# A gated recurrence with a capped choice of experts: exponentials moved ahead of the last decay, register loads in parts of 16 and 8, products in gaps, front and zeros rearranged

## The chip, the cores and the metric

One core of one Trainium2 chip runs the whole program. The metric is device time in microseconds of one execution. The kernel before has a median of 233.89 us over 3 runs (233.44 to 235.4).

## The reference

Two blocks follow each other. The first is a recurrence over 5056 steps for 4 batches and 256 channels, the second a layer of 8 experts of which each keeps the 80 tokens with the largest gate weight; all other rows of the output are zero.

```python
sig = 1 / (1 + exp(-f_logit)); f = lower_bound + (1 - lower_bound) * sig
for t in range(S):                       # S = 5056, h is (4, 256)
    h = f[:, t] * h + (1 - f[:, t]) * x[:, t];  y[:, t] = h
x = y.reshape(20224, 256)
logits = x @ w_gate                      # (20224, 8)
expert = argmax(logits); gate = softmax(logits)[expert]
for e in range(8):                       # the 80 best tokens of expert e
    tok = tokens of e with the 80 largest gate
    out[tok] = gate[tok] * (relu(x[tok] @ w1[e]) @ w2[e])   # 256 -> 1024 -> 256
```

All arithmetic is float32. The inputs x and f_logit are 20.7 MB each, the expert weights 16.8 MB, the output 20.7 MB.

## The kernel before, in words

**The loop.** The sequence is cut into 10 groups of 512 steps (the last has 448), and each group into 4 units, one per batch: 40 units. For each unit SyncE's queue (SP) loads 512 KB of f_logit and 512 KB of x into one of 4 buffers each, three units ahead (`load`, L243). ScalarE (ACT) takes the sigmoid in place (`gate`, L252), GpSimd (POOL) multiplies x with it (`enter`, L256), TensorE (PE) transposes both to channels (`to_channels`, L263), ACT makes the decay from the transposed sigmoid (`decay`, L273), and VectorE (DVE) runs the recurrence as a scan (`scan`, L281) into `h_all`, which holds all states in SBUF, channels down the partitions. PE makes the gate logits of the unit before (`logits`, L296). When the 4 units of a group are done, ACT copies its logits out of PSUM (`aside`, L304), PE turns them to tokens (`by_token`, L310), DVE subtracts the maximum (`maxima`) and marks the chosen expert (`choice`, the last step of which, L337, is on POOL). The four engines work through these steps in the order in which the program writes them; each engine's instructions run in order, and nothing is reordered. Each DMA that SP issues uses one of eight semaphores in turn and waits for the DMA eight before it.

**The zeros.** The output has to be zero where no token is kept. One megabyte of zeros is written to a scratch tensor (`z_dram`, `spread_zeros`, L240), from where SP copies it to the output in quarters of a chunk (32 partitions x 2048 numbers, 256 KB, `clear_some`, L164): 14 quarters in the loop, 6 behind the last load, 30 between the first six weight loads and 30 behind the other weight loads, 80 in all.

**The choice of tokens.** After the loop the shifted logits are exponentiated and summed (`exponentials` L343, `halved` L357, `sums` L349), the gate weight's reciprocal is put in a list per expert (`worth` L371, `turned` L377, `candidates` L383), and the best 12 of each of 128 lists are found (`peaks` L388, `vals` L536 and L539). A product with `spread` (`rivals`, L549) lets every candidate be compared with those of the other lists (`signs` L559 on ACT, `beat` L578 on DVE); those with less than 80 above them are kept, and their places in `h_all` are written to `trow` (L605), one row of 80 numbers per expert. `busy` (L178) issues products of the identity with itself, whose result nobody reads: 16 behind `rivals` and 22 behind `kept`.

**The gathers.** For each expert three engines share the 80 tokens (`gather`, L664 and L669): each loads some numbers of the expert's row of `trow` into registers with one TENSOR_LOAD per part, and then copies, number by number, 2 x 4 bytes per partition from `h_all` to `xe`. DVE then scales `xe` to `xt` (`scaled`, L677). The parts before are 18 and 16 on DVE, 14 and 14 on ACT, 18 on POOL.

**The experts.** Each expert has 8 pieces of `hidden` (two products each, L701) and 8 of `result` (L716), the latter 6 pieces behind; ACT applies the relu per half expert (L710), DVE scales the result (L731), POOL scatters it to the output (L734). The weights are loaded in halves of 512 KB (32 of them) into a ring of 6 buffers: SP issues the next when PE has used one up, and with it 1 or 2 quarters of zeros (`more`). The scatters wait until all zeros are issued.

Of the kernel before, what the change touches and what calls it, by code (L numbers as in the profile page):

```python
# [35 lines left out]
def kernel(  # L36
# [56 lines left out]
    lb = consts.tile([P, DC], F32, name="lb")  # L93
    nc.scalar.dma_start(out=lb, in_=lower_bound.rearrange("(o p) -> p o", p=P))
# [3 lines left out]
    nc.scalar.dma_start(out=wg[:, :, :E], in_=w_gate.rearrange("(o p) e -> p o e", p=P))  # L98
# [54 lines left out]
    z_dram = dram.tile([P, ZR * D], F32, name="z_dram")  # L153
# [4 lines left out]
    zeros = [(k, q) for k in clears for q in range(ZQ)]  # L158


    def clear(k, q=0, m=ZQ):
        n = min(ZR, N // P - k) * D
        rows = ds(q * QP, m * QP)
        nc.sync.dma_start(out=out_z[rows, ds(k * D, n)], in_=z_dram[rows, :n])  # L164
# [34 lines left out]
    with tc.tile_pool(name="ld", bufs=4) as ld, \  # L199
# [6 lines left out]
        def setup():  # L206
# [26 lines left out]
            nc.vector.tensor_scalar(omlb, lb, -1.0, 1.0, ALU.mult, ALU.add)  # L233
            nc.vector.tensor_scalar(nomlb, lb, 1.0, -1.0, ALU.mult, ALU.add)
            for o in range(DC):
                nc.vector.tensor_scalar_mul(wg[:, o], wg[:, o], omlb[:, ds(o, 1)])

        def spread_zeros():
            m = ZR * D // ZC
            nc.sync.dma_start(out=z_dram.rearrange("p (m z) -> p m z", m=m),  # L240
                              in_=zero.unsqueeze(1).broadcast_to([P, m, ZC]))
# [162 lines left out]
        LAST = n_unit - 1  # L404

        for n in range(-AHEAD, n_unit):
            unit(load, n + AHEAD)
            if n == -1:
                spread_zeros()
# [7 lines left out]
            if n == LAST - 2:  # L417
                aside(OLD)
            elif n == LAST - 1:
                exponentials(0, OLD)  # L420
            unit(scan, n)
            some_of(of_group, 1)
            unit(logits, n - 1)
            if n + AHEAD == LAST:
                clear_some(6)
            elif B <= n < n_unit - 2 * B and n % 2:
                clear_some(1)
            if n > 0 and n % B == 0:
# [19 lines left out]
        candidates(HALF)
# [11 lines left out]
        turned(g, 1, fresh[:, ds(NP * TOP + P, P)])  # L460
        for k in (2, OLD - 2, HALF):
# [71 lines left out]
    with tc.tile_pool(name="sel", bufs=1) as sel:  # L533
# [18 lines left out]
        busy(psu, 16, "up")  # L552
# [307 lines left out]
```

## Time and profile before

| | us |
|---|---|
| median of 3 runs | 233.89 |
| runs | 233.44 to 235.4 |
| profiled execution: its own time | 233.3 |
| its span, first to last instruction | 231.5 |
| busy PE / DVE / ACT / POOL | 191.3 / 156.0 / 134.4 / 130.6 |
| mean granted clock of PE | 0.934 |
| moved by DMA | 81.58 MB, mean 352 GB/s |

Times in the rows below are from the start of the span. A row of the timeline has the start, the time from the first to the last of the merged instructions, the engine, the line, the operation, the tiles (out <- in), the count, and in brackets how long the engine was idle before and what ended that. PE's weight loads (PEld) run beside its products. A granted clock of 1.00 is 2.4 GHz, 0.50 is 1.2 GHz.

### The profile page before, as it was taken

The numbers are of one execution on the slowest core, as the hardware profiler recorded it, in microseconds if no ns is written. First come the engines' busy times: TensorE is split into PE (matmuls) and PEld (weight loads), VectorE is DVE, ScalarE is ACT, GpSimd is POOL, SyncE is SP. The second block draws the span as 40 slices with busy tenths as digits, with TensorE's granted clock in tenths as the row PEclk, the third lists the DMA queues.
The fourth block names the chain that finished last, engine by engine and source line by source line (L and its number), as shares of the span: only waits on it lengthen the run. The fifth ranks groups of instructions, "written<-read, shape, count | busy, mean of one in ns | idle before, by whom it ended". The sixth has DMA issues, their size and how long they took to land.

```text
span 231.5 us, 5464 instructions
## 1 busy us (share of the span) xinstructions
PE 191.3 (83%) x1825; PEld 160.9 (69%) x1825; DVE 156.0 (67%) x503; ACT 134.4 (58%) x399; POOL 130.6 (56%) x229
## 2 busy tenths in 40 slices
PE   0688999998999999999995619849899799889990
PEld 0676878788787878787874409849778577657860
DVE  5468779998999999999999479342562544253010
ACT  4457879888888888878766307055564165340110
POOL 2359788888989898989783601044434431300731
PEclk9997999999999999999999656995599999999997
DMA  5999999999999999999975999952389999999920
GB/s 165 394 416 420 417 421 418 417 415 418 418 415 423 417 420 418 420 415 420 405 302 195 379 367 367 379 219 77 143 277 395 405 405 405 415 400 401 385 83 25
DMA packets 29188, 81.58 MB, mean 352 GB/s; under 512 B 3296, under 2 KB 11616, under 8 KB 26720
## 3 DMA queue, kind: packets, MB, share of 16 engines
q1 hardware_dynamic: 28224, 80.49, 88.5%
q0 software_dynamic: 384, 0.66, 0.9%
q8 instruction: 16, 0.26, 0.4%
q14 instruction: 20, 0.16, 0.2%
q10 hardware_dynamic: 544, 0.01, 0.1%
HBM read 79.44 MB, written 22.41 MB: 440 GB/s over the span
## 4 chain that ended last, share of the span: by engine, by line
DMA 38%; PE 28%; ACT 10%; DVE 7%; issue 6%; POOL 5%; DVEq 2%; ACTq 0%; POOLq 0%; SPq 0%
DMA f_t<-in_f_logit_dram 17%; DMA out_dram<-z_dram 7%; PE sp L263 7%; DMA w_sb<-in_moe_w_dram 7%; PE y_ps L716 5%; PE lg L296 5%; ACT h_all L273 4%; DMA x_t<-in_x_dram 4%; DVE xe L669 4%; PE up L263 3%; PE h_ps L701 3%; POOL x_t L256 3%; DMA wg<-in_moe_w_gate_dram 3%; ACT f_t L252 3%; PE warm L178 2%
## 5 line engine op out<-in xcount | busy, mean ns | idle before, releaser
L256 POOL TENSOR_TENSOR x_t<-f_t,x_t 128x1024 f32<-128x1024 f32 x39 | 92.3, 2375 | 19.4 <-DMA x_t<-in_x_dram 16.1
L281 DVE TENSOR_TENSOR_SCAN h_all<-h_all,up 128x512 f32<-128x512 f32 (+1 forms) x80 | 94.7, 1241 | 5.8 <-ACT h_all L273 4.3
L273 ACT ACTIVATE h_all<-sp,nomlb 128x512 f32<-128x512 f32 (+1 forms) x80 | 50.1, 676 | 14.2 <-PE sp L263 14.1
L263 PE MATMUL sp<-ident,f_t 128*128 128x128 f32 x320 | 46.1, 289 | 7.0 <-ACT f_t L252 5.8
L701 PEld LDWEIGHTS h_ps<-xt,w_sb 128*128 128x128 f32 x256 | 40.3, 208 | 14.1 <-DVE xt L677 4.5
L252 ACT ACTIVATE f_t<-f_t 128x1024 f32<-128x1024 f32 x40 | 42.5, 1062 | 12.1 <-DMA f_t<-in_f_logit_dram 12.1
L263 PE MATMUL up<-ident,x_t 128*128 128x128 f32 x320 | 43.6, 281 | 4.3 <-POOL x_t L256 2.6
L263 PEld LDWEIGHTS sp<-ident,f_t 128*128 128x128 f32 x320 | 36.5, 146 | 15.1 <-issue 12.5
L669 DVE COPY xe<-h_all 128x8 uint8 x272 | 22.0, 164 | 34.6 <-issue 34.6
L701 PE MATMUL h_ps<-xt,w_sb 128*128 128x80 f32 x256 | 40.0, 287 | 5.9 <-DVE xt L677 3.9
L263 PEld LDWEIGHTS up<-ident,x_t 128*128 128x128 f32 x320 | 37.1, 144 | 6.6 <-POOL x_t L256 4.5
L716 PE MATMUL y_ps<-w_sb,hid 128*80 128x256 f32 x128 | 38.6, 392 | 3.7 <-issue 1.7
L669 POOL COPY xe<-h_all 128x8 uint8 x144 | 19.4, 195 | 36.6 <-issue 17.8
L669 ACT COPY xe<-h_all 128x8 uint8 x224 | 23.7, 193 | 23.7 <-issue 23.5
L296 PE MATMUL lg<-h_all,wg 128*32 128x128 f32 (+1 forms) x640 | 26.9, 285 | 4.5 <-ACT ls L304 2.9
L296 PEld LDWEIGHTS lg<-h_all,wg 128*32 128x32 f32 x640 | 15.6, 109 | 11.7 <-ACT ls L304 4.8
L734 POOL DMA_INDIRECT out_dram<-y,goal x8 | 7.5, 938 | 20.8 <-DMA w_sb<-in_moe_w_dram 15.2
L710 ACT ACTIVATE hid<-h_ps 128x320 f32<-128x320 f32 x16 | 6.9, 433 | 21.1 <-PE h_ps L701 17.7
L716 PEld LDWEIGHTS y_ps<-w_sb,hid 128*80 128x80 f32 x128 | 15.1, 156 | 5.5 <-issue 3.2
L731 DVE TENSOR_SCALAR y<-y_ps,gsl 80x256 f32<-80x256 f32 x8 | 3.8, 476 | 12.5 <-PE h_ps L701 8.0
L178 PEld LDWEIGHTS warm<-ident 128*128 128x128 f32 x76 | 10.3, 220 | 0.1
L178 PE MATMUL warm<-ident 128*128 128x128 f32 x76 | 10.4, 303 | 0.0
(125 smaller groups left out, 97.3 us busy)
## 6 DMA issues: line engine op xcount, KB each, us to landing
f_t<-in_f_logit_dram SPq DMA_DIRECT2D x40, 512.0 KB, 6.6
x_t<-in_x_dram SPq DMA_DIRECT2D x40, 512.0 KB, 7.0
w_sb<-in_moe_w_dram SPq DMA_DIRECT2D x32, 512.0 KB, 7.7
out_dram<-z_dram SPq DMA_DIRECT2D x31, 256.0 KB, 7.0
out_dram<-z_dram SPq DMA_DIRECT2D x10, 512.0 KB, 9.0
out_dram<-z_dram SPq DMA_DIRECT2D x4, 1024.0 KB, 15.1
out_dram<-z_dram SPq DMA_DIRECT2D x3, 768.0 KB, 9.1
z_dram<-zero SPq DMA_DIRECT2D x1, 1024.0 KB, 8.9
```

What stands on the lines that cost most here:

```text
L178: nc.tensor.matmul(warm, ident, ident, start=True, stop=True)
L252: nc.scalar.activation(s_t, s_t, ACT.Sigmoid, scale=-1.0)
L256: (nc.gpsimd if n else nc.vector).tensor_tensor(u_t, sts[n], u_t, ALU.mult)
L263: nc.tensor.transpose(at, src[n][:, r, ds(o * P, P)], ident)
L273: nc.scalar.activation(columns(n, o).rearrange("c (p r) -> c p r", r=R), sps.pop((n, o)).rearrange("c (r p) -> c p r", r=R) [:, lead(n // ...
L281: nc.vector.tensor_tensor_scan(h, h, ups.pop((n, o))[:, lead(n // B):], columns(n - B, o)[:, size(n // B - 1) - 1:] if n >= B else 0.0, AL ...
L296: nc.tensor.matmul(lgs[g][ds(r * LC, LC), b, :k], wg[:, o], h[:, r], start=o == 0, stop=o == DC - 1, skip_group_check=True)
L669: copy(xe[:, :, ds(WORD * (k + j), WORD)], pair(v - HOME))
L701: nc.tensor.matmul(HP[e, i][:, c], w[1, e, i][:, o, ds(c * P, P)], XT[e][:, o], start=o == 0, stop=o == DC - 1, skip_group_check=True)
L710: nc.scalar.activation(HID[e][:, ds(i * CH, CH)], HP.pop((e, i)), ACT.Relu)
L716: nc.tensor.matmul(YP[e], HID[e][:, c], w[2, e, c // CH][:, c % CH], start=c == 0, stop=c == FC - 1)
L734: one = nc.gpsimd.indirect_dma_start(out=out, out_offset=bass.IndirectOffsetOnAxis(ap=goal[:, ds(e, 1)], axis=0), in_=Y.pop(e), in_offset= ...
```

## The change

It has six parts. (1) The exponentials of groups 0 to 7 stand ahead of the last unit's decay on ACT, their sums (`halved`) are all on POOL, right behind the last `enter`, the choice of group 8 moves behind the last scan, wholly to DVE, and the copy of the last logits (`aside(9)`) comes ahead of the candidates. (2) `busy` gets 16 more products at the start, 4 ahead of the last `by_token`, 32 behind the last `turned`, and 20 instead of 16 behind `rivals`. (3) The parts of the gathers are 16 and 16 on DVE, 16 and 8 on ACT, 16 and 8 on POOL. (4) `lb` is loaded as two rows of 128 numbers and transposed by PE; `w_gate` is loaded by SP behind the second unit, and scaled behind the first scan. (5) The first megabyte of zeros goes straight to the output and is copied from there; `z_dram` is gone. (6) Of the 76 quarters left 20 are issued in the loop (also behind every unit from 28 to 35), 6 behind the last load, 30 with the first six weights, 20 with the next 16 weights (1, and 2 with every fourth).

```diff
-PAD = 40
+PAD = 48
...
-    lb = consts.tile([P, DC], F32, name="lb")
-    nc.scalar.dma_start(out=lb, in_=lower_bound.rearrange("(o p) -> p o", p=P))
+    lb = consts.tile([DC, P], F32, name="lb")
+    nc.scalar.dma_start(out=lb, in_=lower_bound.rearrange("(o p) -> o p", p=P))
...
-    zeros = [(k, q) for k in clears for q in range(ZQ)]
+    zeros = [(k, q) for k in clears[1:] for q in range(ZQ)]
+
+    def first_zeros(zero):
+        m = ZR * D // ZC
+        nc.sync.dma_start(out=out_z[:, :ZR * D].rearrange("p (m z) -> p m z", m=m),
+                          in_=zero.unsqueeze(1).broadcast_to([P, m, ZC]))
...
-        nc.sync.dma_start(out=out_z[rows, ds(k * D, n)], in_=z_dram[rows, :n])
+        nc.sync.dma_start(out=out_z[rows, ds(k * D, n)], in_=out_z[rows, :n])
...
-            nc.vector.tensor_scalar(omlb, lb, -1.0, 1.0, ALU.mult, ALU.add)
-            nc.vector.tensor_scalar(nomlb, lb, 1.0, -1.0, ALU.mult, ALU.add)
+            busy(psu, 16, "up")
+            lb_t = plg.tile([P, DC], F32, name="lb_t", tag="lt")
+            nc.tensor.transpose(lb_t, lb, ident[:DC, :DC])
+            nc.vector.tensor_scalar(omlb, lb_t, -1.0, 1.0, ALU.mult, ALU.add)
+            nc.vector.tensor_scalar(nomlb, lb_t, 1.0, -1.0, ALU.mult, ALU.add)
+
+        def gates():
             for o in range(DC):
                 nc.vector.tensor_scalar_mul(wg[:, o], wg[:, o], omlb[:, ds(o, 1)])
...
             if n == LAST - 2:
                 aside(OLD)
+                exponentials(0, OLD)
             elif n == LAST - 1:
-                exponentials(0, OLD)
+                for k in range(0, OLD, HALF):
+                    halved(k, HALF)
             unit(scan, n)
-            some_of(of_group, 1)
+            if n == 0:
+                gates()
+            some_of(of_group, 1 if n != LAST - 1 else 0)
...
-            elif B <= n < n_unit - 2 * B and n % 2:
+            elif B <= n < LAST - AHEAD and (n % 2 or n >= n_unit - 3 * B):
                 clear_some(1)
...
-        halved(0, HALF)
-        sums(HALF, OLD)
-        worth(0, 0, 2, nc.gpsimd)
-        candidates(0)
+        aside(g)
+        busy(psu, 4, "up")
+        by_token(g)
+        for k in (0, 2, HALF):
+            worth(k, k // HALF * HALF, 2, nc.gpsimd)
         worth(OLD - 2, HALF, 2, nc.vector)
-        aside(g)
-        worth(2, 0, 2, nc.gpsimd)
-        candidates(2)
-        by_token(g)
-        candidates(OLD - 2)
-        worth(HALF, HALF, 2, nc.gpsimd)
-        candidates(HALF)
+        for k in (0, 2, OLD - 2, HALF):
+            candidates(k)
...
         turned(g, 1, fresh[:, ds(NP * TOP + P, P)])
+        busy(psu, 32, "up")
...
-        busy(psu, 16, "up")
+        busy(psu, 20, "up")
...
-    ways = [(mybir.EngineType.DVE, nc.vector.tensor_copy, [18, 16]),
-            (mybir.EngineType.Activation, nc.scalar.copy, [14, 14]),
-            (mybir.EngineType.Pool, nc.gpsimd.tensor_copy, [K - 62])]
+    ways = [(mybir.EngineType.DVE, nc.vector.tensor_copy, [16, 16]),
+            (mybir.EngineType.Activation, nc.scalar.copy, [16, 8]),
+            (mybir.EngineType.Pool, nc.gpsimd.tensor_copy, [16, K - 72])]
...
-                    clear_some(1 + len(late) % 2)
+                    clear_some(1 + (len(late) % 4 == 0))
```

In the built program `trow` begins at byte 24224 of a partition's memory before, and at byte 24704 after: `lb`, which stands ahead of it, takes 512 bytes where it took 8, rounded up to 32. The row of an expert begins there in the expert's partition, and a part at column k begins 4k bytes further.

Three places show how instructions move. On ACT, at the end of the loop, before (`f_t` is the sigmoid, `h_all` the decay, `ls` the copied logits, `cand` the shifted logits):

```order
L252 ACTIVATE f_t<-f_t 128x1024
L273 ACTIVATE h_all<-sp,nomlb 128x448 x2
L304 COPY ls<-lg 128x512
L273 ACTIVATE h_all<-sp,nomlb 128x448 x2
L343 ACT_TABLE_LOAD
L343 ACTIVATE cand<-cand 128x1024
L343 ACTIVATE cand<-cand 128x128
L383 COPY cand<-ct 128x256
L304 COPY ls<-lg 128x4x112
L383 COPY cand<-ct 128x256 x3
```

and now:

```order
L255 ACTIVATE f_t<-f_t 128x1024
L276 ACTIVATE h_all<-sp,nomlb 128x448 x2
L307 COPY ls<-lg 128x512
L346 ACT_TABLE_LOAD
L346 ACTIVATE cand<-cand 128x1024
L276 ACTIVATE h_all<-sp,nomlb 128x448 x2
L346 ACTIVATE cand<-cand 128x128
L307 COPY ls<-lg 128x4x112
L386 COPY cand<-ct 128x256 x4
```

The large exponential and its table load moved ahead of the last decay, and the last copy of logits ahead of the four copies of candidates. On PE, from the last logits to the first expert, before (`ct` and `fresh` are turned candidates, `warm` the products that nobody reads):

```order
L296 MATMUL lg<-h_all,wg 32x112 x24
L377 MATMUL ct<-ident,gm 128x128 x4
L310 MATMUL lt<-ident,ls 128x128 x4
L377 MATMUL ct<-ident,gm 128x128 x4
L377 MATMUL fresh<-ident,gm 128x128 x2
L549 MATMUL rivals<-spread,mates 128x192 x2
L178 MATMUL warm<-ident 128x128 x16
L586 MATMUL sums_p<-count,before 128x1
L602 MATMUL kept<-put,what 16x80 x12
L178 MATMUL warm<-ident 128x128 x22
```

and now:

```order
L299 MATMUL lg<-h_all,wg 32x112 x24
L181 MATMUL warm<-ident 128x128 x4
L313 MATMUL lt<-ident,ls 128x128 x4
L380 MATMUL ct<-ident,gm 128x128 x8
L380 MATMUL fresh<-ident,gm 128x128 x2
L181 MATMUL warm<-ident 128x128 x32
L555 MATMUL rivals<-spread,mates 128x192 x2
L181 MATMUL warm<-ident 128x128 x20
L592 MATMUL sums_p<-count,before 128x1
L608 MATMUL kept<-put,what 16x80 x12
L181 MATMUL warm<-ident 128x128 x22
```

The turn of the last logits (`lt`) moved ahead of all candidates, and 32 products stand between the last candidates and `rivals`. On POOL, the end of the gathers now reads:

```order
L670 TENSOR_LOAD trow
L675 COPY xe<-h_all 128x2x4 x16
L670 TENSOR_LOAD trow
L675 COPY xe<-h_all 128x2x4 x8
L740 DMA out_dram<-y,goal 20224x256 x4
L670 TENSOR_LOAD trow
L675 COPY xe<-h_all 128x2x4 x16
L670 TENSOR_LOAD trow
L675 COPY xe<-h_all 128x2x4 x8
L740 DMA out_dram<-y,goal 20224x256 x4
```

Before, each expert had one load and 18 copies there, and all eight scatters stood behind the last of them; now four scatters stand ahead of the last expert's gather.

## Rows read from the trace of the kernel before

**Rows 1.** The page: the chain that ended last, share of the span by engine.

```profile
DMA 38%; PE 28%; ACT 10%; DVE 7%; issue 6%; POOL 5%; DVEq 2%; ACTq 0%; POOLq 0%; SPq 0%
```

**Rows 2.** The page: GB/s of the DMA engines in 40 slices of 5.79 us.

```profile
GB/s 165 394 416 420 417 421 418 417 415 418 418 415 423 417 420 418 420 415 420 405 302 195 379 367 367 379 219 77 143 277 395 405 405 405 415 400 401 385 83 25
```

**Rows 3.** Stretches: busy PE, PEld, DVE, ACT, POOL; then PE's clock, DMA share, GB/s.

```profile
130.00:135.00 5.00, 2.51 (x10) 1.52 (x8) 3.37 (x12) 1.22 (x4) 1.88 (x6) 0.50 1.02 363
145.00:150.00 5.00, 4.32 (x48) 4.13 (x47) 1.37 (x6) 0.21 (x1) 0.00 (x0) 1.00 0.99 381
160.00:165.00 5.00, 4.19 (x18) 3.67 (x18) 1.65 (x17) 3.18 (x29) 2.44 (x19) 0.50 0.47 161
```

**Rows 4.** Timeline, SP's queue in the front.

```profile
5.92 0.63 SPq L240 DMA_DIRECT2D z_dram<-zero  x1
```

**Rows 5.** Timeline, ACT and DVE at the end of the loop.

```profile
117.06 1.06 ACT L252 ACTIVATE f_t<-f_t 128x1024 f32<-128x1024 f32 x1 [0.35 <-DMA f_t<-in_f_logit_dram]
119.24 0.59 ACT L304 COPY ls<-lg 128x512 f32<-128x512 f32 x1
121.90 1.16 ACT L273 ACTIVATE h_all<-sp,nomlb 128x448 f32<-128x448 f32 x2 [2.08 <-PE sp L263]
123.08 1.28 ACT L343 ACT_TABLE_LOAD   x1
...
123.90 2.17 DVE L281 TENSOR_TENSOR_SCAN h_all<-h_all,up 128x448 f32<-128x448 f32 x2
...
124.37 1.26 ACT L343 ACTIVATE cand<-cand 128x1024 f32<-128x1024 f32 x2
```

**Rows 6.** Timeline, the choice of tokens.

```profile
128.79 0.54 ACT L304 COPY ls<-lg 128x448 f32<-128x448 f32 x1
...
133.20 0.47 PE L377 MATMUL fresh<-ident,gm 128*128 128x128 f32 x1 [0.56 <-DVE gm L367]
...
138.00 0.36 DVE L544 TENSOR_TENSOR spread<-vals,place 128x192 f32<-128x192 f32 x1
...
138.56 1.62 PE L549 MATMUL rivals<-spread,mates 128*128 128x192 f32 x4 [4.89 <-DVE spread L544]
```

**Rows 7.** Timeline, 22 products (two instructions each) and the write of trow.

```profile
147.71 5.18 PE L178 MATMUL warm<-ident 128*128 128x128 f32 x44
147.82 0.23 DVE L605 TENSOR_SCALAR trow<-kept 8x80 int32<-8x80 f32 x1 [1.33 <-PE kept L602]
```

**Rows 8.** Register loads of line 664: duration ns min/median/max, start; five parts of one row.

```profile
L664 DVEq TENSOR_LOAD <-trow x1: 1573/1573/1573, 173.6 to 173.6; - x1
L664 DVEq TENSOR_LOAD <-trow x1: 3617/3617/3617, 165.9 to 165.9; - x1
L664 ACTq TENSOR_LOAD <-trow x1: 3062/3062/3062, 172.9 to 172.9; - x1
L664 ACTq TENSOR_LOAD <-trow x1: 1217/1217/1217, 162.0 to 162.0; - x1
L664 POOLq TENSOR_LOAD <-trow x1: 4043/4043/4043, 168.7 to 168.7; - x1
```

**Rows 9.** Timeline, the first gathers and the first expert.

```profile
152.62 2.38 POOL L669 COPY xe<-h_all 128x8 uint8 x18 [10.01 <-issue]
...
154.27 1.33 DVE L669 COPY xe<-h_all 128x8 uint8 x16 [2.86 <-issue]
...
156.11 4.93 PE L701 MATMUL h_ps<-xt,w_sb 128*128 128x80 f32 x24 [3.22 <-DVE xt L677]
...
162.92 0.42 ACT L710 ACTIVATE hid<-h_ps 128x320 f32<-128x320 f32 x1
```

**Rows 10.** The chain in order of time: start, us, what; the experts.

```profile
174.63 0.43 PE y_ps L716 x2
175.07 0.40 PE h_ps L701 x4
...
225.29 0.49 DVE y L731
```

More of the change, by code (lines that the diff above doesn't have):

```diff
@@ L97 @@
     nc.vector.memset(wg, 0.0)
-    nc.scalar.dma_start(out=wg[:, :, :E], in_=w_gate.rearrange("(o p) e -> p o e", p=P))
     omlb = consts.tile([P, DC], F32, name="omlb")
@@ L152 @@
     ZC = 512
-    z_dram = dram.tile([P, ZR * D], F32, name="z_dram")
     out_z = out.rearrange("(p k) d -> p (k d)", p=P)
@@ L232, in setup @@
             nc.vector.tensor_tensor(before, before, mates, ALU.mult)
-            nc.vector.tensor_scalar(omlb, lb, -1.0, 1.0, ALU.mult, ALU.add)
-            nc.vector.tensor_scalar(nomlb, lb, 1.0, -1.0, ALU.mult, ALU.add)
+            busy(psu, 16, "up")
[4 more added lines that the diff above has]
+        def gates():
             for o in range(DC):
                 nc.vector.tensor_scalar_mul(wg[:, o], wg[:, o], omlb[:, ds(o, 1)])
[L238 to L241, printed above, removed]
         def load(n):
@@ L404 @@
         LAST = n_unit - 1
+        HALF = OLD // 2
         for n in range(-AHEAD, n_unit):
             unit(load, n + AHEAD)
-            if n == -1:
-                spread_zeros()
+            if n == -2:
+                nc.sync.dma_start(out=wg[:, :, :E], in_=w_gate.rearrange("(o p) e -> p o e", p=P))
+            elif n == -1:
+                first_zeros(zero)
             if n == -AHEAD:
@@ L430 @@
                 of_group += ([[lambda g=g: aside(g)]] if g < OLD else [])
-                of_group += [[lambda g=g: shifted(g)], [lambda g=g: choice(g, nc.gpsimd)]]
+                of_group += [[lambda g=g: shifted(g)], [lambda g=g: choice(g, nc.gpsimd if g < OLD else nc.vector)]]
         assert not of_group
@@ L435 @@
         g = n_grp - 1
-        HALF = OLD // 2
-        halved(0, HALF)
-        sums(HALF, OLD)
-        worth(0, 0, 2, nc.gpsimd)
-        candidates(0)
-        worth(OLD - 2, HALF, 2, nc.vector)
-        aside(g)
-        worth(2, 0, 2, nc.gpsimd)
-        candidates(2)
-        by_token(g)
-        candidates(OLD - 2)
-        worth(HALF, HALF, 2, nc.gpsimd)
-        candidates(HALF)
+        aside(g)
[3 more added lines that the diff above has]
+            worth(k, k // HALF * HALF, 2, nc.gpsimd)
+        worth(OLD - 2, HALF, 2, nc.vector)
+        for k in (0, 2, OLD - 2, HALF):
+            candidates(k)
         assert OLD == 8
@@ L824 @@
             nc.vector.tensor_scalar(trow, rp, float(WORD), float(HOME), ALU.mult, ALU.add)
-            for k in clears:
+            zero = sel.tile([P, ZC], F32, name="zero")
+            nc.vector.memset(zero, 0.0)
+            first_zeros(zero)
+            for k in clears[1:]:
                 clear(k)
```

## The prediction

> **What bounds the kernel now.** I read the chain of waits by engine first [rows 1]: DMA holds 38% of it, PE 28%. The throughput by slices [rows 2] shows two stages in which the 16 DMA engines are the limit (about 418 GB/s from 12 to 110 us, about 400 from 174 to 220) and a hole between (slices of 77 to 302). So the program has three parts with three limits: the loop over 40 units (transfers), the choice of tokens and the first gathers (waits between engines), the experts (PE, held up by transfers). The table of stretches [rows 3] shows PE at 0.50 of its clock (1.2 GHz) in 130 to 135 and 160 to 165, and at 1.00 (2.4 GHz) in 145 to 150. Three marks: A, the end of the copy of group 8's logits, 119.24 + 0.59 = 119.83 [rows 5]; T, the end of the write of `trow`, 147.82 + 0.23 = 148.05 [rows 7]; and the end of PE's work, 225.29, where DVE starts on the last y [rows 10]. From there to the execution's own 233.3 are 8.0 us, which no edit touches. That execution lies 0.6 under the median of 233.89; 1% is 2.3 us, about what the measurement can tell.
>
> **Zeros, loop.** A quarter chunk is 32 x 2048 x 4 B = 0.262 MB. The loop issues 20 of them where it issued 14, the six more in the stretch where the loads run closest; the first megabyte goes to the output in place of `z_dram`, the same bytes. The queue is full there (405 to 423 GB/s from 12 to 116 us [rows 2]), and the sigmoid of the last unit waited 0.35 us for its f_t [rows 5], so nothing hides the bytes: 6 x 0.262 / 0.418 = **+3.8** on A. Bounds: 0 if the compute of those units had the slack, 3.8.
>
> **Front.** The zeros' first write was issued at 5.92 [rows 4], behind the 4-byte pieces of `lb`, whose completion it waited for. `lb` is now two rows of 512 B. The first two slices lack (417 - 165) and (417 - 394) GB/s x 5.79 us = 1.6 MB, 3.8 us, most of it the start itself. I take **-0.5**, between 0 and -1.8. The 16 products and the transpose ahead of the first f_t are PE time while PE waits for the second f_t anyway; up to +1 if the first release of a buffer is late, inside that range. `gates` on DVE moves past two scans: before the first logits, free.
>
> **Exponentials.** Table load and exponential are 1.28 + 1.07 us: 123.08 to 125.4 [rows 5], after the last decay. Now they start at A = 119.83 and end at 122.2; the last decay, ready at 121.90 [rows 5], starts 0.3 late. DVE doesn't feel it: its scan before runs until 123.5, and the last scan, which now doesn't follow the choice of group 8, starts 0.45 us earlier than 123.90 [rows 5]. The table load had no visible gap behind it (1.28 us, the exponential at +1.29). The Trainium skill's page "ScalarE: Activation LUTs", section "What ACT_TABLE_LOAD costs", adds a drain of about 1.38 us to each load, which speaks against the move: by it the last decay would start 1.7 late and the last scan some 0.7 late. The trace shows no such drain behind this load, so the sum goes without.
>
> **Last logits.** Their copy stood at 128.79 [rows 6], behind the exponentials, a POOL sum and another copy, 2.7 us after the last scan's end (126.07). Now it waits for the choice of group 8 on DVE, an exponential of 128 and the last logits: about 0.8 us. But the peaks of the first pair still go ahead on DVE. The transpose that ends the chain moves from 133.20 to about 131.4 [rows 6]: -1.8.
>
> **32 products.** They are put behind that transpose. 22 took 5.18 us at full clock [rows 3, 7], 0.235 each, so 32 take 7.5: 131.6 to **139.1**. `spread` is then ready at 136.6 (138.36 - 1.8) [rows 6], and the product of rivals, queued behind, waits for them: 139.1 instead of 138.56. If PE is at 1.2 GHz for part of it (0.50 in 130 to 135 [rows 3]), up to 142.5; I take 139.9, since PE has four more products and no gap over 1 us until 128.7. From the rivals to T were 9.5 us; 0.8 goes because the rivals' 1.62 us [rows 6] were at half clock. T before the loop's shift: 139.9 + 8.7 = 148.6: **+0.5** (-0.8 to +2.6). Without the wait behind the products it would be -2.
>
> **Register loads.** The decisive part. [Rows 8] give five loads of one expert's row of `trow`: 18 numbers from column 0 in 1.57 us, 16 from 18 in 3.62, 14 from 34 in 3.06, 14 from 48 in 1.22, 18 from 62 in 4.04. That is 0.087 us a number for the first and fourth, 0.22 for the others, whatever the engine or count. The tile began at byte 24224 of its partition; the fast parts begin at bytes that 32 divides (24224, 24416), the slow ones not (24296, 24360, 24472). Now it begins at 24704 (`lb` has grown by 480 bytes), and all parts (columns 0, 16, 32, 48, 56, 72) at bytes that 32 divides. I price all at 0.087: 1.40 for 16, 0.70 for 8. Bounds: 0.087 and 0.225.
>
> First gather: DVE's second load started 0.76 us before its copies were done, so it shows 0.64 where it showed 2.86 [rows 9]. DVE: 1.40 + 0.5 (as POOL's first: 152.62 - 148.05 - 4.04 [rows 8, 9]) + 1.33 + 0.64 + 1.33 = T + 5.2; POOL: 1.9 + 24 copies of 0.132 (2.38 / 18) = T + 5.1. Then xt: PE starts at **T + 5.6** instead of 8.06 [rows 9], 0.75 us behind its 22 products (end T + 4.8) instead of 3.2.
>
> Its first y needs the first relu on ACT, at T + 14.9 [rows 9], behind three slow loads that now are 1.66 shorter each: T + 10.5, y at 10.95. From there 57 pieces of h at 0.40 and 64 of y at 0.43 [rows 10] are 50.3: T + 61.3. The same count for before gives T + 65.7 against 77.2 measured, so 11.5 us were lost, part of it at 1.2 GHz (0.50 in 160 to 165 [rows 3]), the rest in waits for xt, for weights and for DVE's y. What is lost now: PE still pauses some 2 us before that first y, after h pieces alone, so I expect a spell at 1.2 GHz: 2.0 (0 to 5). Weights: 26 x 0.524 + 20 quarters = 18.6 MB instead of 21.2. At 0.40 MB/us from T + 7.2 the last lands at T + 55, ahead of PE; but all zeros go with the first 16 weights, 13.4 MB, so the 16th lands near T + 43.5; PE without waits asks for it 37 pairs after its first y, at T + 42. I take 2.7 in all (0 to 7). PE's end: **T + 66.0** instead of 77.2, **-11.2**.
>
> **Sum.** +3.8 - 0.5 + 0.5 - 11.2 = -7.4: 233.3 - 7.4 = 225.9, against the median 226.5. I say **226**.
>
> **The rivals.**
> (a) Flat price per register. If a number costs 0.22 wherever the part begins, DVE needs per expert 2 x (3.0 + 1.3) + 0.8 for xt and y, 9.4 us, over PE's 8 x 0.83 = 6.7, and decides from there: the eighth xt comes at T + 10 + 7 x 9.4 = 76, PE ends at T + 85, the kernel near 245, **slower**. Against it: two of five parts cost 0.087, on DVE and on ACT. The Trainium skill says this flat price: "Runtime: NRT & Kernel Launch", section "Instruction fetch mechanics", has about 200 ns a register even in bulk. The trace agrees with it in three loads of five (0.22) and not in two (0.087). 5%; POOL alone staying at 0.22 (its only load was slow, so engine and place are not apart there) makes 24 x 0.22 = 5.3 us of loads, of which some 3.2 show beside 3.2 of copies, 6.4 us per expert, and about 230: 7%.
> (b) Half clock. The 32 products and the first experts run at 1.2 GHz as 130 to 135 and 160 to 165 did [rows 3]: +2.6 and +3: 231. For it: the pauses; against: they are shorter. 13%.
> (c) The loop hides the six quarters: -3.3, 222.5. Against it the full queue. 12%.
> (d) Little comes of it: weights late as before (+6), products +2.6: 234 to 236. For it: even with 10 quarters less in the expert stage the queue stays full up to the 16th weight. 8%.
> My forecast keeps 55%. A small one inside it: POOL now issues four scatters ahead of the last gather, and these wait for the last zeros (near T + 45); the last xt is then due about when PE asks, within 2 us.
>
> Range: **220** (c with the lower bounds of clock and waits) to **232** (b). Faster by over 1% (under 231.5): 55 + 12 + 7 + two thirds of (b) and a little of (d), **0.84**; within 1%: **0.09**; slower: (a) and half of (d), **0.07**.
>
> **What would show it.** Register loads near 1.4 and 0.7 us on all three engines; first h 5 to 6 us behind `trow`, first y near 11. The last f_t 3 us later, so the last scan ends near 129. Rivals directly behind the 32 products, with `spread` done over 2 us before. In the experts, xt every 6 to 7 us and fewer waits for weights. I am wrong if the loads of POOL stay over 3 us, if the hole in the throughput is no shorter, or if the last f_t comes no later.

## The result and the profile after

The kernel after takes 226.30 us, the median of 4 runs (224.88 to 228.33); the kernel before took 234.18 in the 4 runs beside them. The ratio is 0.9638, with a 95% interval of 0.9569 to 0.9707: faster by 3.6%. (The ratio leaves out the run of 228.33, which is 1.5% above the fastest and counts as slow.) 226 was predicted. The profiled execution took 226.11, 7.2 less than that of before (233.3).

The page, with the chain by engine, PE's granted clock and GB/s in 40 slices (of 5.6 us):

```profile
DMA 44%; PE 31%; ACT 11%; DVE 4%; POOL 3%; issue 2%; SPq 1%; POOLq 1%; ACTq 0%; DVEq 0%
PEclk9999999999999999999999999999999999999998
GB/s 227 341 417 415 420 420 415 417 421 417 419 416 421 417 421 417 422 415 425 414 418 386 91 324 392 385 361 398 201 292 319 408 400 411 399 379 378 284 21 23
```

Against [rows 1, 2] DMA's share of the chain has grown from 38% to 44%. The loop is as full as before. The hole behind the choice of tokens, 219, 77, 143 and 277 before, is now 201 and 292; the one behind the last loads, 302 and 195 before, has become deeper, 91 and 324. The clock is whole throughout, also in the stretches of [rows 3] (busy PE, PEld, DVE, ACT, POOL; PE's clock, DMA share, GB/s), two of which stood at 0.50:

```profile
130.00:135.00 5.00, 2.49 (x17) 1.66 (x15) 3.35 (x11) 1.54 (x5) 2.62 (x8) 1.00 0.93 310
145.00:150.00 5.00, 4.21 (x44) 3.96 (x43) 2.54 (x14) 2.13 (x9) 0.00 (x0) 1.00 1.01 345
160.00:165.00 5.00, 5.00 (x39) 4.40 (x38) 3.61 (x43) 2.57 (x19) 5.00 (x37) 1.00 0.91 317
```

In the front the first megabyte of zeros is issued 1.75 us earlier than in [rows 4]; the timeline of SP:

```profile
4.17 0.40 SPq L160 DMA_DIRECT2D out_dram<-zero  x1
```

The end of the loop, timeline of ACT, DVE and POOL [rows 5]:

```profile
120.65 1.06 ACT L255 ACTIVATE f_t<-f_t 128x1024 f32<-128x1024 f32 x1 [0.98 <-DMA f_t<-in_f_logit_dram]
122.64 0.58 ACT L307 COPY ls<-lg 128x512 f32<-128x512 f32 x1
123.25 1.28 ACT L346 ACT_TABLE_LOAD   x1
124.54 1.06 ACT L346 ACTIVATE cand<-cand 128x1024 f32<-128x1024 f32 x1
125.50 1.14 ACT L276 ACTIVATE h_all<-sp,nomlb 128x448 f32<-128x448 f32 x2
129.44 0.53 ACT L307 COPY ls<-lg 128x448 f32<-128x448 f32 x1
...
124.60 4.25 DVE L284 TENSOR_TENSOR_SCAN h_all<-h_all,up 128x448 f32<-128x448 f32 x4
...
125.68 3.14 POOL L360 TENSOR_TENSOR cand<-cand 128x256 f32<-128x256 f32 x6 [1.28 <-ACT cand L346]
```

The last sigmoid starts 3.6 us later than before and waits 0.98 for its f_t. The first mark (A, the end of the copy of group 8's logits) is 122.64 + 0.58 = 123.22, where before had 119.83. The exponential is followed at once by the last decay.

The choice of tokens [rows 6, 7], PE and DVE:

```profile
135.09 0.33 PE L380 MATMUL fresh<-ident,gm 128*128 128x128 f32 x1 [1.21 <-DVE gm L370]
135.26 7.31 PE L181 MATMUL warm<-ident 128*128 128x128 f32 x64
142.41 0.82 PE L555 MATMUL rivals<-spread,mates 128*128 128x192 f32 x4
...
139.75 0.36 DVE L550 TENSOR_TENSOR spread<-vals,place 128x192 f32<-128x192 f32 x1
150.72 0.23 DVE L611 TENSOR_SCALAR trow<-kept 8x80 int32<-8x80 f32 x1 [1.33 <-PE kept L608]
```

`spread` is ready at 140.11, but the rivals start at 142.41, behind the 32 products: a wait of 2.3 us. `trow` is written at 150.95 (T), 2.9 later than before, though A is 3.4 later.

Register loads (duration in ns, min/median/max over 16 each) [rows 8]. DVE's parts are all of 16 numbers; on ACT and POOL the maximum is a 16, the minimum an 8:

```profile
L670 POOLq TENSOR_LOAD <-trow x16: 562/841/1281, 151.0 to 204.5; - x16
L670 DVEq TENSOR_LOAD <-trow x16: 1097/1098/1354, 151.0 to 194.8; - x16
L670 ACTq TENSOR_LOAD <-trow x16: 542/784/1222, 151.0 to 196.7; - x16
```

The first gathers and the first expert [rows 9]:

```profile
152.43 1.28 DVE L675 COPY xe<-h_all 128x8 uint8 x16 [1.48 <-issue]
154.11 1.33 DVE L675 COPY xe<-h_all 128x8 uint8 x16 [0.40 <-issue]
...
156.32 2.90 PE L707 MATMUL h_ps<-xt,w_sb 128*128 128x80 f32 x24 [0.53 <-DVE xt L683]
158.74 0.43 ACT L716 ACTIVATE hid<-h_ps 128x320 f32<-128x320 f32 x1
159.96 0.60 PE L722 MATMUL y_ps<-w_sb,hid 128*80 128x256 f32 x2
```

The load between DVE's two parts now shows 0.40 us where it showed 2.86. From T to the first h are 5.4 us instead of 8.1, to the first y 9.0.

The chain in order of time, end of the experts [rows 10]:

```profile
189.32 8.21 DMA w_sb<-in_moe_w_dram
197.53 0.14 issue
197.67 0.64 PE h_ps L707 x4
198.31 0.43 PE y_ps L722 x2
...
217.30 0.49 DVE y L737
```

and PE's waits from 150 us on, the first of the list (us in total, times, longest):

```profile
PE h_ps L707 <- DMA w_sb<-in_moe_w_dram: 3.9, 5, 1.0
```

Up to 197.5 the chain goes through weights and zeros, from there PE runs without a gap to 217.30, which is T + 66.35, where before had T + 77.24.

### The profile page after: what moved, and what is told of

It is laid out like the page before. It is cut to its first block, busy times and chain, and to the rows that moved or that the text cites. A ratio compares the mean times of both kernels' runs of the same rounds, so it can differ in the third digit from the quotient of the medians.

```text
span 224.2 us, 5701 instructions
## 1 busy us (share of the span) xinstructions
PE 194.8 (87%) x1938; PEld 165.1 (74%) x1938; DVE 157.7 (70%) x487; ACT 131.6 (59%) x367; POOL 139.8 (62%) x279
## 4 chain that ended last, share of the span: by engine, by line
DMA 44%; PE 31%; ACT 11%; DVE 4%; POOL 3%; issue 2%; SPq 1%; POOLq 1%; ACTq 0%; DVEq 0%
DMA f_t<-in_f_logit_dram 21%; DMA w_sb<-in_moe_w_dram 11%; DMA x_t<-in_x_dram 9%; PE warm L181 7%; PE h_ps L707 6%; PE y_ps L722 6%; PE sp L266 5%; ACT h_all L276 4%; DMA out_dram<-out_dram 3%; ACT f_t L255 3%; PE lg L299 3%; PE up L266 3%; ACT ls L307 2%; ACT signs L565 2%; POOL xe L675 1%
## 5 line engine op out<-in xcount | busy, mean ns | idle before, releaser
L707 PEld LDWEIGHTS h_ps<-xt,w_sb 128*128 128x128 f32 x256 | 37.0, 191 | 12.4 <-issue 5.2
L266 PE MATMUL sp<-ident,f_t 128*128 128x128 f32 x320 | 43.8, 280 | 1.5 <-ACT h_all L276 1.5
L266 PEld LDWEIGHTS up<-ident,x_t 128*128 128x128 f32 x320 | 35.3, 140 | 10.1 <-POOL x_t L259 9.3
L266 PEld LDWEIGHTS sp<-ident,f_t 128*128 128x128 f32 x320 | 34.4, 141 | 9.5 <-issue 6.9
L707 PE MATMUL h_ps<-xt,w_sb 128*128 128x80 f32 x256 | 36.5, 268 | 4.9 <-DMA w_sb<-in_moe_w_dram 3.9
L722 PE MATMUL y_ps<-w_sb,hid 128*80 128x256 f32 x128 | 37.3, 381 | 0.0
L675 POOL COPY xe<-h_all 128x8 uint8 x192 | 26.2, 197 | 12.8 <-issue 8.2
L675 DVE COPY xe<-h_all 128x8 uint8 x256 | 20.9, 162 | 11.4 <-issue 11.3
L181 PE MATMUL warm<-ident 128*128 128x128 f32 x188 | 24.9, 298 | 1.4 <-POOL ident masks.py:199 1.4
L181 PEld LDWEIGHTS warm<-ident 128*128 128x128 f32 x188 | 24.3, 213 | 1.7 <-POOL ident masks.py:199 1.4
L675 ACT COPY xe<-h_all 128x8 uint8 x192 | 20.2, 193 | 5.4 <-issue 3.4
```

The costliest lines, as they stand in the source:

```text
L181: nc.tensor.matmul(warm, ident, ident, start=True, stop=True)
L266: nc.tensor.transpose(at, src[n][:, r, ds(o * P, P)], ident)
L675: copy(xe[:, :, ds(WORD * (k + j), WORD)], pair(v - HOME))
L707: nc.tensor.matmul(HP[e, i][:, c], w[1, e, i][:, o, ds(c * P, P)], XT[e][:, o], start=o == 0, stop=o == DC - 1, skip_group_check=True)
L722: nc.tensor.matmul(YP[e], HID[e][:, c], w[2, e, c // CH][:, c % CH], start=c == 0, stop=c == FC - 1)
```

## The experiments

One table for all, worked out from rows like those above. A is the end of the copy of group 8's logits, T the end of the write of `trow`, PE's end the start of DVE's last y; "tail" is the profiled execution's own time less PE's end; these four come from one profiled execution of each kernel. "Zeros" are the quarters in the loop / behind the last loads / with the first six weights / behind the others. Ratios are to the runs of the kernel before that were made beside each kernel.

| kernel | zeros | A | T - A | PE's end - T | tail | median | ratio (interval) |
|---|---|---|---|---|---|---|---|
| before | 14/6/30/30 | 119.83 | 28.22 | 77.24 | 8.0 | 234.18 | 1 |
| after | 20/6/30/20 | 123.22 | 27.73 | 66.35 | 8.8 | 226.30 | 0.9638 (0.9569-0.9707) |
| x1_shift | 20/6/30/20 | 123.24 | 29.07 | 90.73 | 8.3 | 251.40 | 1.0732 (1.0656-1.0808) |
| x2_parts | 14/6/30/30 | 120.23 | 27.65 | 69.83 | 8.0 | 226.02 | 0.9642 (0.9584-0.9701) |
| x3_none | 20/6/30/20 | 123.82 | 27.53 | 65.63 | 8.5 | 225.14 | 0.9596 (0.9536-0.9656) |
| x4_loop14 | 14/6/30/26 | 120.08 | 29.42 | 67.64 | 8.4 | 226.14 | 0.9679 (0.9594-0.9764) |
| x5_hole | 14/12/30/20 | 119.69 | 29.22 | 65.71 | 8.6 | 223.35 | 0.9522 (0.9484-0.9559) |
| x6_post8 | 20/12/36/8 | 123.35 | 29.34 | 60.66 | 7.9 | 222.57 | 0.9512 (0.9459-0.9565) |
| x7_exp | 20/6/30/20 | 123.29 | 33.08 | 66.32 | 7.9 | 230.88 | 0.9851 (0.9786-0.9917) |
| x8_mix | 8/12/36/20 | 118.38 | 25.99 | 69.11 | 8.3 | 222.66 | 0.9496 (0.9458-0.9533) |
| x9_prod16 | 20/6/30/20 | 123.50 | 25.99 | 65.36 | 8.1 | 223.21 | 0.9516 (0.9457-0.9574) |
| x10_mix14 | 14/12/36/14 | 119.76 | 26.04 | 67.05 | 8.2 | 221.22 | 0.9427 (0.9383-0.9472) |
| x11_mix42 | 14/12/42/8 | 119.59 | 26.05 | 70.70 | 8.2 | 224.52 | 0.9563 (0.9519-0.9606) |
| x12_even | 14/12/33/17 | 119.95 | 26.06 | 61.56 | 11.4 | 219.89 | 0.9385 (0.9347-0.9423) |

**Where a part of the row begins, alone.** Edit to the kernel after:

```diff
-PAD = 48
+PAD = 40
...
-    trow = consts.tile([E, K], I32, name="trow")
+    trow = consts.tile([E, K + TOP], I32, name="trow")[:, ds(2, K)]
```

The tile grows by 32 bytes, and the pad behind it shrinks by as many, so that nothing else moves.

> The kernel after, with `trow` begun 8 bytes further on, so that each part begins 8 bytes behind a multiple of 32; counts (16 and 8) and everything else stay. My theory (the place decides): 0.22 us a number, so 3.6 us for 16 and 1.8 for 8 on all three engines where the kernel after has 1.1 and 0.55; DVE then needs 2 x (3.6 + 1.3) + 0.8 = 10.6 us per expert against 6.7 of PE, the first h comes 9 to 11 us behind `trow` instead of 5.4, PE's end 90 to 100 behind it instead of 66, the run takes 248 to 260. Rival (the count decides: 16 and 8 are cheap, 14 and 18 dear): the loads stay at 1.1 and 0.55, the run at 226.

The loads of this kernel:

```profile
L670 POOLq TENSOR_LOAD <-trow x16: 1827/2715/3831, 152.3 to 227.0; - x16
L670 DVEq TENSOR_LOAD <-trow x16: 3603/3616/4053, 152.4 to 226.8; - x16
L670 ACTq TENSOR_LOAD <-trow x16: 1746/2810/3646, 152.4 to 218.2; - x16
```

and its first h in the timeline:

```profile
162.27 1.14 PE L707 MATMUL h_ps<-xt,w_sb 128*128 128x80 f32 x4 [5.12 <-DVE xt L683]
```

The same numbers in the same parts on the same engines, 8 bytes further on: 3.6 us instead of 1.1 for 16, 1.8 instead of 0.55 for 8. The first h comes 10.0 us behind T, PE's end 90.7, the kernel 25 us slower than the kernel after. The theory of the place holds with all its numbers; that of the count falls. This is the rival (a) of the prediction, made to happen.

**The parts alone.** Edit to the kernel before:

```diff
-    ... [18, 16]), ... [14, 14]), ... [K - 62])]
+    ... [16, 16]), ... [16, 8]), ... [16, K - 72])]
```

> The kernel before, with only the parts of the register loads changed: 16 and 16 on DVE, 16 and 8 on ACT, 16 and 8 on POOL, all beginning at multiples of 32 bytes as its `trow` does. My theory (the parts carry nearly all of the gain): loads of 1.1 and 0.55 us, first h about 5.5 us behind `trow`, first y 9 to 10, PE's end 67 to 71 behind it (a spell at 1.2 GHz and ten quarters of zeros more than the kernel after has there) instead of 77.2; 148 + 69 + 8 = 225, between 222 and 229. Rival (weights and zeros hold the experts, not the loads): the first h comes earlier but PE waits for weights instead, 230 to 234.

Its loads, and its first h in the timeline:

```profile
L664 POOLq TENSOR_LOAD <-trow x16: 563/812/1285, 147.9 to 182.0; - x16
L664 DVEq TENSOR_LOAD <-trow x16: 1097/1100/1365, 147.9 to 192.1; - x16
L664 ACTq TENSOR_LOAD <-trow x16: 544/788/1225, 147.9 to 194.5; - x16
```

```profile
153.28 2.90 PE L701 MATMUL h_ps<-xt,w_sb 128*128 128x80 f32 x24 [0.56 <-DVE xt L677]
```

Three lists of numbers give 0.9642, the whole change 0.9638. The first h stands 5.4 us behind T, PE's end 69.8. This kernel has ten quarters of zeros more behind its weights, and PE's end is 3.5 further from T than in the kernel after (69.83 against 66.35); that is about what the loop of the kernel after pays for its six (its A is 3.0 to 3.6 later than in the kernels with 14). So the other five parts of the change come to nothing together in the time, within the intervals. (With the places of the parts this edit also changes their lengths and the shares of the engines: 32 numbers on DVE for 34, 24 on ACT for 28, 24 on POOL for 18. What the lengths and shares are worth by themselves was not tried; x1_shift, which keeps them, shows that the place alone is enough for a larger effect.)

**No products ahead of the rivals.** Edit to the kernel after:

```diff
         turned(g, 1, fresh[:, ds(NP * TOP + P, P)])
-        busy(psu, 32, "up")
```

> The kernel after, without the 32 products behind the last `turned`. First theory (the products only stand in the way of the rivals): the rivals' product starts with `spread`, 140.2 instead of 142.4, `trow` is written 2.2 us earlier, PE stays at the full clock, the run takes 224. Second theory (they hold the clock): PE is at 0.5 of its clock from about 136 to 145 as in the kernel before, the rivals take 1.6 instead of 0.8 us, `trow` comes only 0 to 1.4 us earlier, and a spell at 0.5 may come in the first experts too: 225 to 229.

A stretch (columns as above), and the rivals in the timeline, of the kernel without the products:

```profile
140.00:145.00 5.00, 3.96 (x16) 3.99 (x17) 4.86 (x13) 2.78 (x11) 1.06 (x4) 0.50 1.04 398
```

```profile
141.04 1.62 PE L554 MATMUL rivals<-spread,mates 128*128 128x192 f32 x4 [4.89 <-DMA out_dram<-out_dram]
```

The second theory, in its milder form: the rivals follow `spread` at once, but PE stands at 0.50 and they take 1.62 instead of 0.82. T - A is 27.53 against 27.73 in the kernel after, whose 32 products ran at the full clock, and 29.1 to 29.4 in x1_shift, x4_loop14, x5_hole and x6_post8, where the first of them ran at 0.50. So 32 products take away at least what the clock gives. A spell in the experts did not come. The medians (225.14 and 226.30) are within each other's intervals.

**Sixteen products instead of 32.** Edit to the kernel after: `busy(psu, 16, "up")` at that place.

> The kernel after, with 16 identity products instead of 32 behind the last `turned`. First theory (16 are enough for the clock and end before `spread`): the rivals start 0.2 to 0.6 us behind `spread` (140.5 where the kernel after had 142.4) and take 0.8 to 0.9, `trow` comes 25.9 to 26.2 behind the copy of group 8's logits instead of 27.7, 224 to 224.8. Second theory (the 16 run at 0.5 of the clock, as the first of the 32 did in five of the seven runs that have them): they take 7 us, the rivals start as late as before, 226.

The timeline of PE:

```profile
135.54 3.74 PE L181 MATMUL warm<-ident 128*128 128x128 f32 x32
140.60 0.89 PE L555 MATMUL rivals<-spread,mates 128*128 128x192 f32 x4 [1.32 <-DMA w_sb<-in_moe_w_dram]
```

(The text on record counts wrongly: six kernels have the 32, and five of them show less than the full clock there.) First theory: the 16 end 1.3 us before the rivals, the rivals start 0.2 behind `spread` at the full clock, T - A falls by 1.74. The time, 223.2, is below the expected 224 to 224.8: in the profiled execution PE's end is also 1.0 closer to T and the tail 0.7 shorter, for which no reason was found.

The full clock is not certain with 16 either. They took 3.7 us here and in x8_mix, but 5.4 in the other three kernels that have 16; in x10_mix14 (clock 0.57 in 132 to 136):

```profile
131.85 5.37 PE L181 MATMUL warm<-ident 128*128 128x128 f32 x32
```

Even so they are over about when `spread` is ready, and T - A is 25.99 to 26.06 in all five: 1.5 less than without products, 1.7 to 3.4 less than with 32.

**The exponentials back behind the last decay.** Edit to the kernel after:

```diff
                 aside(OLD)
-                exponentials(0, OLD)
             elif n == LAST - 1:
+                exponentials(0, OLD)
                 for k in range(0, OLD, HALF):
```

> The kernel after, with the exponential of the first eight groups back behind the last decay. First theory (with the last logits' copy put first, the exponential has to come early): table and exponential run from 126.7 to 129.0 instead of 123.25 to 125.6, POOL's sums end at 132.1 instead of 128.8, everything up to the last transpose 2 to 3.3 later, `trow` at 153 to 154, the run at 228 to 229.5; the last decay 0.3 earlier is worth nothing. Second theory (PE's and ACT's own order holds the chain, the sums are not late): 226.

Timelines of ACT, POOL and PE:

```profile
126.44 1.28 ACT L346 ACT_TABLE_LOAD   x1
127.73 1.06 ACT L346 ACTIVATE cand<-cand 128x1024 f32<-128x1024 f32 x1
...
128.87 3.23 POOL L360 TENSOR_TENSOR cand<-cand 128x256 f32<-128x256 f32 x6 [4.01 <-ACT cand L346]
...
137.82 0.47 PE L380 MATMUL fresh<-ident,gm 128*128 128x128 f32 x1 [1.11 <-DVE gm L370]
138.08 9.91 PE L181 MATMUL warm<-ident 128*128 128x128 f32 x64
147.83 0.82 PE L555 MATMUL rivals<-spread,mates 128*128 128x192 f32 x4
```

First theory, and more than it expected: POOL's sums start 3.2 us later (128.87 against 125.68), the last transpose 2.7 later, and the 32 products, begun when PE's clock already stood at 0.50 (from 134 us on, by the granted clock), take 9.9 instead of 7.3. Together T - A grows by 5.35. That is against the kernel after, whose 32 ran at the full clock; against the kernels whose 32 ran in part at 0.50 (29.1 to 29.4) it grows by 3.7 to 4.0.

**Where the zeros go.** Three kernels with the 32 products of the kernel after and other places for the 76 quarters. First the loop as before, six more behind the experts' weights (two with every second one):

```diff
-            elif B <= n < LAST - AHEAD and (n % 2 or n >= n_unit - 3 * B):
+            elif B <= n < n_unit - 2 * B and n % 2:
...
-                    clear_some(1 + (len(late) % 4 == 0))
+                    clear_some(1 + len(late) % 2)
```

> The kernel after, with 14 quarters of zeros in the loop as in the kernel before, and six more (26) behind the weights of the experts, two with every second one. My theory (the six cost 0.6 us each where the queue is full): the copy of group 8's logits ends at 119.7 instead of 123.2, `trow` at 147.5 instead of 151; the six go to the experts, where the queue is full as well until the 16th weight, so that PE's end goes from 66.4 to 68 to 70 behind `trow`: 224 to 226. Rival (DVE, 0.97 busy in the loop, is the limit once the six are gone): the mark comes only 1 to 2 us earlier, 226 to 229. Second rival (the experts hide zeros): 222.7.

A is 3.1 earlier, as the first theory has it, and PE's end 1.3 further from T. That the run isn't faster than the kernel after (226.14) comes from this 1.3 and from the 32 products: they took 8.9 us here, so T - A is 1.7 longer. Then the same loop, but the six into the pause behind the last loads:

```diff
-                clear_some(6)
+                clear_some(12)
```

> The kernel after, with 14 quarters of zeros in the loop and 12 instead of 6 behind the last loads (in the 4 us in which the transfers pause before the first weights); 20 stay behind the experts' weights. First theory (that pause takes six quarters for nothing): the copy of group 8's logits ends at 120.1, the first weights land no later, PE's end is 66 to 66.5 behind `trow`: 222.5 to 224.5. Second theory (the six delay the weights): the same mark at 120.1, but the wait for weights in the experts grows by the 3 us won: 226.

The pause takes them for nothing: A 119.69, PE's end 65.7 behind T instead of 67.6, 223.35. Next the kernel after with 12 in that pause, 6 with each of the first six weights (`clear_some(6)` for `clear_some(5)`) and 8 left for the experts:

> The kernel after, with 20 quarters in the loop as there, 12 instead of 6 behind the last loads, 6 instead of 5 with each of the first six weights, and so 8 instead of 20 behind the experts' weights. First theory (the zeros behind the weights cause PE's waits of 7 us): marks up to `trow` stay (151), PE's end comes 61 to 63 behind it instead of 66.4, the run takes 220.5 to 223. Second theory (the weights' own bytes, and xt, cause them): 65 to 66, 225 to 226. The write of `trow` could be later by 0 to 1 if more transfers run beside the choice of tokens.

PE's longest waits from 150 us on in this kernel:

```profile
PE kept L608 <- DVE put L604: 0.7, 1, 0.7
PE h_ps L707 <- DVE xt L683: 0.6, 1, 0.6
```

No wait for a weight is left, and PE's end is 60.7 behind T: the waits of the kernel after came, all or nearly all, from the zeros between the weights. (T is 1.7 later here, which gives the weights as much more time; PE's end comes 5.7 closer.) Its `trow` is later than expected, since its 32 products too ran at 0.66 of the clock (135 to 140).

**Adding them up.** Loop 8 (`n % B == 1`), 12, 36, 20, with 16 products:

> The kernel after, with 8 quarters of zeros in the loop, 12 behind the last loads, 36 with the first six weights, 20 behind the others, and 16 identity products instead of 32 ahead of the rivals. First theory (each quarter out of the loop is worth 0.57 us until DVE is the limit): the copy of group 8's logits ends at 117 to 119, `trow` 27.5 behind it, PE's end 66 behind that: 219.5 to 222.5. Second theory (with 14 quarters the loop is at DVE's limit already): 119.5 to 120, 223 to 224.

T comes at 144.4, 6.6 earlier, but PE's end is 69.1 behind it: 2.8 of the 6.6 is given back in the experts. And from 14 to 8 quarters A wins only 1.2 to 1.7, where 20 to 14 won about 3.6. The traces point to the engines: with 8 quarters the queue is no longer full all the time. From 40 to 60 us (columns as above), first with 8, then with 14 (x10_mix14):

```profile
40.00:60.00 20.00, 19.16 (x240) 16.44 (x238) 19.00 (x23) 17.17 (x25) 17.51 (x10) 1.00 0.99 392
40.00:60.00 20.00, 18.92 (x235) 16.00 (x234) 19.14 (x23) 16.68 (x25) 17.26 (x10) 1.00 1.02 417
```

From 15 to 118 us ACT's waits for f_t's transfers fall from 11.2 to 6.0 us in all. Which engine holds the loop then was not settled. Then 14/12/36/14 and 14/12/42/8, each with 16 products:

> The kernel after, with 14 quarters of zeros in the loop, 12 behind the last loads, 36 with the first six weights, 14 behind the others, and 16 products. First theory (the four effects add): the copy of group 8's logits ends at 119.7, `trow` 26.2 behind it at 146, PE's end 62 to 64 behind that, 216.5 to 218.5. Second theory (all transfers from that copy to the end are one queue, and earlier compute only waits longer in the experts, as with 8 quarters in the loop): PE's end 66 to 67 behind `trow`, 220 to 222.

> As the kernel with 14 quarters in the loop, 36 with the first six weights and 14 behind the others, but 42 and 8. First theory (the hole in the transfers 7 to 12 us behind `trow` takes six more for nothing): PE's end 61 to 63 behind `trow`, 216 to 217.5, about 1 less than that kernel. Second theory (the 7th weight queues behind them and lands after PE asks for it, some 14 us behind `trow`): a single wait of 2 to 4 us there, 218 to 220.

Both first theories fall. With 14/12/36/14 PE's end is 67 behind T and the time 221.2, as its second theory has it. With 42 PE's end is 70.7, and there most of what is lost is one wait (timeline of PE):

```profile
169.03 1.11 PE L722 MATMUL y_ps<-w_sb,hid 128*80 128x256 f32 x2 [6.41 <-DMA w_sb<-in_moe_w_dram]
```

This is the kind of wait that the second theory has for this kernel, but 6.4 us instead of 2 to 4, and it ends 23.4 behind T, so that the time is 224.5 instead of 218 to 220. The 7th weight stands in the queue behind the zeros that were sent with the first six. So the last kernel sends less with these (33) and the 17 that are left evenly:

```diff
-        clear_some(5)
+        clear_some(6 if key != order[RING - 1] else 3)
...
-                    clear_some(1 + (len(late) % 4 == 0))
+                    clear_some(len(late) % 3 > 0)
```

> The kernel after, with 16 products, 14 quarters of zeros in the loop, 12 behind the last loads, 33 with the first six weights, and the last 17 spread evenly, one with two of every three later weights. First theory (PE takes 0.31 MB of weights per us where the transfers bring 0.40, so zeros at an even rate cause no wait): the copy of group 8's logits ends at 119.7, `trow` at 145.8, PE's end 62 to 64 behind it, 216 to 218. Second theory (what is transferred behind that copy is one queue, whatever its order): 66 to 67 behind `trow`, 220 to 221.5.

The timeline of POOL:

```profile
204.09 1.12 POOL L740 DMA_INDIRECT out_dram<-y,goal  x1 [23.66 <-DMA w_sb<-in_moe_w_dram]
...
212.83 0.91 POOL L740 DMA_INDIRECT out_dram<-y,goal  x1 [0.30 <-issue]
```

PE waits for no weight and ends 61.6 behind T, at 207.57, a little before the first theory's 62 to 64; the second theory, one queue whatever its order, falls. But the time is 219.9, not 216 to 218: the scatters wait until all zeros are written (by the code; the trace puts it down to the weights' transfers, which share their queue), the last zeros now go with the 31st of the 32 weights, issued at 197.01, and so all eight are issued 1.2 us apart from 204.09 on, the last 5.3 us behind PE's end. The tail is 11.4 instead of 8 to 9. It is still the fastest kernel here, 0.9385 of before (0.9347 to 0.9423), and its interval lies below that of the kernel after.

## Why the prediction was right, step by step

In the profiled executions A moved by +3.39, T - A by -0.49, PE's end behind T by -10.89 and the tail by +0.81: -7.2 in all, where -7.4 was summed. The main mechanism, the place of the register loads, was right. That the total came so close is in part luck, since several terms were off and cancelled.

**Zeros in the loop, +3.8, and the front, -0.5.** Together +3.3 on A were predicted, +3.39 came. The kernels with 14 quarters and the new front (119.59 to 120.08) lie beside those with 14 and the old one (119.83, 120.23), so the front is worth 0 within 0.4. Between the mean of these five (119.81) and that of the six kernels with 20 quarters (123.40) lie 3.6: each quarter is worth 0.60 where 0.63 was priced. The front wasn't undone by itself.

**Exponentials.** The last decay starts at A + 2.28 (before A + 2.07: 0.2 late, 0.3 predicted), the last scan ends at 128.85, A + 5.63 (before A + 6.24). No drain stands around the table load: the copy before it ends at 123.22, the load takes 123.25 + 1.28, and the exponential begins at 124.54. So the Trainium skill's rule ("ScalarE: Activation LUTs", "What ACT_TABLE_LOAD costs"), by which the last decay would have been 1.7 late, is not borne out by this trace, and the sum was right to leave it out. What the step missed is what the move is for: it was costed at nothing, but without it the choice loses 3.7 to 5.4 us (x7_exp), since the last logits' copy, put first, leaves POOL's sums as the late ones.

**Last logits, -1.8.** The last transpose is at 135.09, A + 11.87, before A + 13.37: -1.5.

**32 products, +0.5.** The mechanism was as predicted: `spread` ready at 140.11, the rivals 2.3 later behind the products. Relative to A, T moved by -0.5. The term was too large by 1.0 for this execution, because the products ran at the full clock (7.3 us), where 7.5 and an addition of 0.8 for half clock in part of them were taken. That addition was not wrong in kind: in the other five kernels that have the 32, the rivals start 8.2 to 9.5 us behind the end of the last transpose instead of 7.0, and in the four of them that leave the choice of tokens as it is T - A is 0.9 to 1.2 over before. The -0.5 was the lucky case. That 16 products would do was not thought of; they are worth 1.7 to 3.4.

**Register loads.** The reason was right: where a part begins sets the price (x1_shift), and the new parts alone make the whole gain (x2_parts). The size was too high: 1.10 and 0.55 us where 1.40 and 0.70 were predicted, 0.069 a number instead of 0.087. The 0.087 came from parts of 18 and 14 [rows 8]. The Trainium skill's "Runtime: NRT & Kernel Launch", "Instruction fetch mechanics", has some 200 ns a register even in bulk; by that the kernel would have been slower. That page speaks of loads from HBM, and these are from SBUF, so it is not a statement on this case, as the prediction took it to be. The price that the traces show is near it where a part begins 8 or 24 bytes behind a multiple of 32 (0.225), and far from it where a part begins on one (0.069).

**Experts, PE's end T + 66.0.** It came at T + 66.35, but out of terms that cancel. First y: T + 9.0 instead of 10.95. The spell at 1.2 GHz, +2.0: none. From the first y to PE's end without waits 50.3 were taken from pieces; x6_post8, which has no wait for weights, shows 213.35 - 161.73 = 51.6. So the kernel after loses 217.30 - 159.96 - 51.6 = 5.7, where 2.7 were predicted; its list of waits shows 3.9 of them for weights and 0.5 for DVE. This term was mis-sized, and its working does not come out: 26 x 0.524 MB and 20 quarters are 18.9 MB, not 18.6, and 13.4 MB at 0.40 MB/us from T + 7.2 land at T + 40.7, not T + 43.5, ahead of the T + 42 at which PE asks, so by that sum there was no wait at all. What it leaves out is the order in the queue: x11_mix42 shows a weight that came 6.4 us late behind zeros issued ahead of it. That the same makes the waits of the kernel after is argued from x6_post8 and x12_even, where fewer or later zeros leave no wait.

**The end, 8.0.** "Which no edit touches" is not so: the tail is 7.9 to 8.8 in all kernels but x12_even, where scatters that are held back make it 11.4.

**Rivals.** (a) did not come, and x1_shift shows what it would have been: 251 (245 was worked out). (b) did not come in the profiled run of the kernel after; its first half, products at half clock, came in the five other kernels that have the 32. (c) did not: the full queue passes the bytes on. (d) did not in full, but waits for weights did: 3.9 us by the list where before had 3.0, so the sign of fewer such waits did not come true. The last xt, at 207.02 behind four scatters, cost PE nothing.

## What to carry to other kernels

Look at the price of a load to registers by the place at which it begins, before its engine or its count: loads of like length of which some cost 2.5 times as much are the sign. Bytes that have to be moved some time cost nothing here in a stretch where the queue was empty, up to the transfer that the next engine waited for (x5_hole, x11_mix42), or evenly between transfers that came faster than they were used (x12_even). And when a change of six parts gives 3.6%, run the parts: here three lists of numbers gave all of it, and other settings of the rest a further 2.6%.

## What the runs showed of the hardware

- A TENSOR_LOAD of 16 int32 numbers from one row takes 1.0 to 1.1 us when it begins at a multiple of 32 bytes and 3.5 to 3.6 when it begins 8 bytes behind one, on DVE, ACT and POOL; of 8 numbers 0.55 and 1.75 to 1.83, on ACT and POOL. In the kernel after the first load of an engine takes 0.2 to 0.3 more (1.35, 1.22, 1.28). In the kernel before, aligned parts of 18 and 14 took 1.57 and 1.22, more than 16; whether a count that is a multiple of 8 is cheaper a number was not tried by itself, nor was a start 16 bytes behind.
- The same 32 products took 7.3, 8.6, 8.9 and 9.9 us in four kernels (after, x1_shift, x4_loop14, x7_exp); the granted clock was 1.00 in the first, 0.50 from 135 to 138 in the second, 0.53 from 133 to 136 in the third, 0.50 from 138 to 142 in the fourth. The first two have the same instructions up to there, and PE began the products at 135.26 and 135.37 behind the same pauses: what made the clock fall in one and not in the other is not shown.
- The half clock of the first expert that [rows 3] show (0.50 in 160 to 165) came back only in x1_shift (0.50 in 165 to 170), where PE again stood still for 5.1 us behind its 22 products. In the kernels whose first h starts 5.4 us behind T, after a pause of 0.5 to 0.6, PE is at 1.00 there.
